# Two layers of a transformer block on one Trainium2 core: the second layer's weight conversions begin at step 28 and stay behind the step that asks for them

## The chip, the core and the metric

The kernel runs on one core of one Trainium2 chip. A core has five engines with a queue each, taken in order: TensorE (PE in the profile, with PEld for its weight loads), VectorE (DVE), ScalarE (ACT), GpSimd (POOL) and SyncE (SP). In this kernel SP and ACT also issue the DMA transfers. The metric is device time in microseconds (us), the median of a few executions; lower is better.

## The reference

A linear attention with a decayed state feeds two feed-forward layers, each with its own weights. All values are float32; the four weight matrices come as float64.

```
for t in range(S):
    state = alpha[:, :, t, :, None] * state + einsum('bhd,bhe->bhde', k[:, :, t], v[:, :, t])
    y[:, :, t] = einsum('bhd,bhde->bhe', q[:, :, t], state)
x = y as (B*S, H*D) = (3072, 384)
h = x @ moe_w_in;   g = h if h >= 1, 0 if h <= -1, else (h + 1)**2 / 4;   x = g @ moe_w_out
h = x @ moe2_w_in;  g = max(0.01 * h, h);                                 out = g @ moe2_w_out
```

Here B = 4, S = 768, H = 8, D = 48, and the hidden width is 2048.

## The kernel before

**Tiles and steps.** The 3072 tokens are 24 chunks of 128, and three chunks make a tile of 384 tokens, so a layer has 8 tiles. A tile of one layer is 16 steps, one for each 128 hidden columns. Layer 1 (layer 0 in the code) is steps 0 to 127, layer 2 is steps 128 to 255. In a step, `gemm_in` makes `h` with nine matmuls (line 451: three row blocks, and three passes each, since every operand is split in a high and a low part), the activation makes the two parts of `gg`, and `gemm_out`, three steps later, adds nine matmuls into three accumulators (line 490 in layer 1, line 492 in layer 2).

**The activation of a step in layer 1** goes round three engines: ACT lines 462 and 463 (read `h`, then square), DVE line 464 (compare with `h`), ACT line 468 (high part of `gg`), POOL line 469 (low part). There are two banks for `h`, so the first matmul of step i+2 waits for line 464 of step i; four buffers of `gg` stand between line 469 and `gemm_out`.

**The attention** of the chunks of the next tile is spread over the 16 steps of a tile. For each chunk: transposes (line 254), scans on DVE (line 269, then after four short instructions line 281), scores (line 320) and their mask on DVE (line 327), the output `y` (lines 365 and 367) and the state (line 341). Its PSUM banks are three in turn, so a score matmul waits until a bank's readers, a scan or a mask, are done. The later tiles of layer 1 have somewhat less of it, the last one and layer 2 none.

**The conversions.** The float64 weights come in 28 pieces a layer. A piece is loaded (line 160; for layer 2 issued on ACT), and converted with integer arithmetic: ACT lines 29 and 30, DVE lines 31 and 32, POOL line 35, DVE line 40. For layer 1 the result is split at once into the resident weights (lines 178 and 182). For layer 2 those weight buffers are still in use, so the converted piece is stored to DRAM (line 187, issued on ACT), and from the last tile of layer 1 on, as each weight buffer comes free, it is loaded again (line 194, on ACT, asked for from step 114) and split.

`tick(layer, n)` does one beat of this: the first part of piece n (`conv_a`: lines 29 to 35), the last part of piece n-1 (`conv_b`: line 40), the load of piece n+2, and the store of piece n-2. Three raw buffers and four `z` buffers carry it; the `z` buffers also take the loads of line 194. Hooks run a tick at a step: for layer 2 the first at step `MF` = 16, then one every `TICK1` = 3 steps.

**What sets the order.** On PE the order is the order of the code. On the other engines a scheduler sets it at build time from its own estimate of when each instruction could start: an instruction whose data it takes to be ready may be queued well ahead of the step in which the code asks for it. The order of a queue is then fixed, and an instruction that has to wait holds up all that stand behind it.

Of the kernel before, what the change touches and what calls it, by code (L numbers as in the profile page):

```python
# [7 lines left out]
F32 = mybir.dt.float32  # L8
# [4 lines left out]
ACTF = mybir.ActivationFunctionType  # L13
ALU = mybir.AluOpType

C = 128
HI, LO = 0, 1
# [45 lines left out]
def fast_path(ctx, tc, q, k, v, alpha, w1i, w1o, w2i, w2o, out, wz, in_range):  # L63
    nc = tc.nc
# [6 lines left out]
    MF = DFF // 128  # L71
# [2 lines left out]
    NCH = NT // C  # L74
    LAG = 3
    TICK1 = 3
    AHEAD = 1
    DQ = 3
    EB = 2
# [16 lines left out]
    op = ctx.enter_context(tc.tile_pool(name="op", bufs=1))  # L96
# [47 lines left out]
    def load_raw(layer, kind, g, i):  # L144
        src = wsrc[layer, kind]
        if kind == "i":
            n = MG * 128
            src = src[i * 128:(i + 1) * 128, g * n:(g + 1) * n]
        else:
            n = DM  # L150
            r0 = (g * MG + i) * 128
            src = src[r0:r0 + 128, :]
        t = rawp.tile([128, MG * 128], I64, tag="raw", name="raw")[:, :n]
        if kind == "i" and layer == 0:
            cols = slice(g * n, (g + 1) * n)
            r3 = KD * R + 32 * i
            (cq if layer else nc.sync).dma_start(out=t[:R], in_=wsrc[layer, kind][i * R:(i + 1) * R, cols])
            (cq if layer else nc.sync).dma_start(out=t[R:], in_=wsrc[layer, kind][r3:r3 + 32, cols])
        else:
            (cq if layer else nc.sync).dma_start(out=t, in_=src)  # L160
        raw[layer, kind, g, i] = t
# [3 lines left out]
    def conv_a(layer, kind, g, i):  # L165
        t = raw.pop((layer, kind, g, i))
        n = t.shape[1]
        z = zp.tile([128, MG * 128], I32, tag="z", name="z")[:, :n]
        half_done[layer, kind, g, i] = to_f32_first(nc, t, z, nc.gpsimd), z

    def conv_b(layer, kind, g, i):
        high, z = half_done.pop((layer, kind, g, i))
        to_f32_last(nc, high, z)
        zs[layer, kind, g, i] = z.bitcast(F32)
# [11 lines left out]
    def store_z(kind, g, i):  # L186
        cq.dma_start(out=wz[kind, g][i], in_=zs.pop((1, kind, g, i)))
# [9 lines left out]
    order = [(kind, g, i) for g in range(NG) for kind in "io" for i in range(KD if kind == "i" else MG)]  # L197
    NO = len(order)

    def tick(layer, n):  # L200
        if n < NO:
            conv_a(layer, *order[n])
        if 0 <= n - 1 < NO:
            conv_b(layer, *order[n - 1])
            if layer == 0:
                split_hi(0, *order[n - 1])
            if n + 2 < NO:
                load_raw(layer, *order[n + 2])
        if 0 <= n - 2 < NO:
            if layer == 0:  # L210
                split_lo(0, *order[n - 2], nc.gpsimd if n % LOP else nc.vector)
            else:
                store_z(*order[n - 2])

    def w_tile(layer, kind, g):
        if (layer, kind, g) not in W:
# [44 lines left out]
    def st_alpha(c):  # L261
        ps = transposed(c, 0)
        if c > 0:
            load_qka(c + AHEAD)
        kt = tp.tile([R, NP, C], F32, tag="kt", name="kt")
# [176 lines left out]
    def gemm_in(layer, j, m, n):  # L442
        N = n * C
        xt = xts[layer, j]
        w = W[layer, "i", m // MG]
        f0 = (m % MG) * 128
        h = ph.tile([128, 512], F32, tag="h", name="h")[:, :N]
        cnt = 0
        for kk in range(KD):
            for wl, xl in PASSES:  # L450
                nc.tensor.matmul(  # L451
                    h, w[:, wl, kk, f0:f0 + 128], xt[:, kk, xl, :],
                    start=cnt == 0, stop=cnt == 3 * KD - 1,
                )
                cnt += 1
        if m == MF - 1:
            xts.pop((layer, j))
        t = ep.tile([128, 384], F32, tag="t", name="t", bufs=EB)[:, :N]
        g = t
        gg = gp.tile([128, 2, 384], F32R, tag="gg", name="gg")[:, :, :N]  # L460
        if layer == 0:
            nc.scalar.activation(out=t, in_=h, func=ACTF.Relu, bias=half, scale=0.5)  # L462
            nc.scalar.activation(out=t, in_=t, func=ACTF.Square)  # L463
            nc.vector.scalar_tensor_tensor(out=g, in0=t, scalar=1.0, in1=h, op0=ALU.min, op1=ALU.max)  # L464
        else:
            nc.scalar.activation(out=t, in_=h, func=ACTF.Copy, scale=0.01)  # L466
            nc.vector.tensor_tensor(out=g, in0=h, in1=t, op=ALU.max)  # L467
        nc.scalar.activation(out=gg[:, HI], in_=g, func=ACTF.Copy)  # L468
        nc.gpsimd.tensor_tensor(out=gg[:, LO], in0=g, in1=gg[:, HI].bitcast(F32), op=ALU.subtract)  # L469
        gs[layer, j, m] = gg  # L470

    def gemm_out(layer, j, m, n):
        N = n * C
# [68 lines left out]
    def at(i, f):  # L542
        hooks.setdefault(i, []).append(f)
# [1 line left out]
    NA = len(tilesA) * MF  # L545
    lastA = NA - MF
    for n in range(3):
        at(MF - 3 + n, lambda n=n: load_raw(1, *order[n]))
    for n in range(NO + 2):
        at(MF + TICK1 * n, lambda n=n: tick(1, n))  # L550
    for n, (kind, g, i) in enumerate(order):
        free = lastA + MG * g + MG + (LAG if kind == "o" else 0)
        at(free + i - 2, lambda a=(kind, g, i): load_z(*a))
# [252 lines left out]
```

## Time and profile before

| | us |
|---|---|
| runs timed | 1044.44 (median of three, 1043.35 to 1045.16) |
| the profiled execution, its own time | 1045.02 |
| span of its trace, first to last instruction | 1043.3 |
| PE busy | 988.5 |
| DVE, ACT, POOL busy | 496.5, 491.6, 399.5 |
| first step of layer 1 begins | 48.4 |
| first step of layer 2 begins | 626.0 |

The span is the time inside the trace; 1.7 us lie around it. The rows further down are of this one execution. A group of instructions in them is named by the line of the kernel, the engine and what it writes and reads, as in "L464 DVE t<-t,h"; "idle before" is how long the engine stood still ahead of such instructions, and behind the arrow stands what ended it.

### The profile page before, as it was taken

Reading aid. Unit: us, or ns where it says so; the run is one execution under the profiler, and the core shown is the slowest. Engines: PE = TensorE matmul, PEld = TensorE weight load, DVE = VectorE, ACT = ScalarE, POOL = GpSimd, SP = SyncE. Lnnn points to the kernel's source line nnn. Section 1 sums busy time; section 2 is a strip of 40 time slices with the busy share of each in tenths; the row PEclk is TensorE's granted clock in tenths of the full one; section 3 lists DMA queues with packets and bytes.
Section 4 is the critical chain, followed back from the end, with each engine's and each line's share of the span. In section 5 each row is a group of like instructions: output and inputs, shape, how many; then the busy total and the mean of one; then the engine's idle time right before and its main releaser. Section 6 shows DMA issues by size and latency. Waiting matters only on the chain.

```text
span 1043.3 us, 15722 instructions
## 1 busy us (share of the span) xinstructions
PE 988.5 (95%) x5874; PEld 963.7 (92%) x5874; DVE 496.5 (48%) x965; ACT 491.6 (47%) x966; POOL 399.5 (38%) x402
## 2 busy tenths in 40 slices
PE   5589799879999999999999999999999999999997
PEld 4588689779999999999999999999999999999997
DVE  7999997886444445354442345241423212221211
ACT  4476666565444444445544674333333333333332
POOL 2477775564233333332222333333333333333332
PEclk9898999999999999999999999999999999999999
DMA  9855558766222121122110235020302000000000
GB/s 191 196 147 134 146 167 239 187 195 166 38 55 46 35 58 35 35 58 42 42 38 6 84 113 170 26 91 2 91 1 68 1 24 1 23 1 23 16 7 27
DMA packets 133652, 78.96 MB, mean 76 GB/s; under 512 B 104384, under 2 KB 122304, under 8 KB 133568
## 3 DMA queue, kind: packets, MB, share of 16 engines
q1 hardware_dynamic: 121472, 52.71, 20.9%
q10 hardware_dynamic: 12096, 25.17, 8.0%
q8 instruction: 48, 0.79, 0.3%
q14 instruction: 36, 0.29, 0.1%
HBM read 59.77 MB, written 15.73 MB: 72 GB/s over the span
## 4 chain that ended last, share of the span: by engine, by line
PE 74%; DVE 11%; DMA 6%; issue 3%; ACT 3%; POOL 2%; SPq 1%; ACTq 0%; POOLq 0%; DVEq 0%
PE h L451 33%; PE acc L492 18%; PE acc L490 14%; DMA raw<-in_moe_w_in 3%; PE y L367 3%; PE sc L320 2%; DVE z L40 2%; DVE z L31 2%; DMA raw<-in_moe_w_out 1%; POOL z L35 1%; PE y L365 1%; DVE z L32 1%; DMA ends<-in_alpha 1%; DVE kt L269 1%; DVE qt L281 1%
## 5 line engine op out<-in xcount | busy, mean ns | idle before, releaser
L451 PE MATMUL h<-xt,wi 128*128 128x384 f32 x2304 | 459.8, 343 | 15.3 <-DVE t L464 7.8
L469 POOL TENSOR_TENSOR gg<-t,gg 128x384 fp32r<-128x384 f32 x256 | 269.1, 1052 | 492.5 <-ACT gg L468 489.3
L451 PEld LDWEIGHTS h<-xt,wi 128*128 128x128 f32 x2304 | 405.9, 189 | 21.9 <-DVE t L464 10.9
L490 PE MATMUL acc<-gg,wo 128*128 128x384 f32 x1152 | 234.6, 347 | 1.9 <-ACT o L503 1.0
L492 PE MATMUL acc<-wo,gg 128*128 128x384 f32 x1152 | 223.5, 338 | 0.0
L468 ACT ACTIVATE gg<-t 128x384 fp32r<-128x384 f32 x256 | 133.6, 522 | 169.9 <-DVE t L464 92.2
L490 PEld LDWEIGHTS acc<-gg,wo 128*128 128x128 f32 x1152 | 202.3, 189 | 5.0 <-ACT o L503 1.3
L492 PEld LDWEIGHTS acc<-wo,gg 128*128 128x128 f32 x1152 | 205.1, 188 | 0.0
L467 DVE TENSOR_TENSOR t<-h,t 128x384 f32<-128x384 f32 x128 | 71.1, 557 | 272.6 <-ACT t L466 272.6
L466 ACT ACTIVATE t<-h 128x384 f32<-128x384 f32 x128 | 62.9, 492 | 180.0 <-PE h L451 178.7
L464 DVE SCALAR_TENSOR_TENSOR t<-t,h 128x384 f32<-128x384 f32 x128 | 70.0, 547 | 119.8 <-ACT t L463 117.3
L462 ACT ACTIVATE t<-h,half 128x384 f32<-128x384 f32 x128 | 73.6, 575 | 81.8 <-PE h L451 63.0
L35 POOL TENSOR_TENSOR z<-z,raw 128x384 int32<-128x384 int32 (+1 forms) x56 | 70.3, 1255 | 66.0 <-DVE z L32 21.3
L463 ACT ACTIVATE t<-t 128x384 f32<-128x384 f32 x128 | 66.8, 522 | 7.0 <-ACT t L462 2.9
L320 PE MATMUL sc<-qab,kt 96*128 96x256 f32 x192 | 53.6, 404 | 14.5 <-DVE S L327 7.4
L367 PE MATMUL y<-S,vpad 128*96 128x128 f32 x384 | 55.9, 272 | 5.6 <-DVE S L327 5.6
L40 DVE SCALAR_TENSOR_TENSOR z<-raw,z 128x384 int32<-128x384 int32 (+1 forms) x56 | 50.8, 909 | 9.8 <-POOL z L35 8.6
L320 PEld LDWEIGHTS sc<-qab,kt 96*128 96x128 f32 x192 | 36.8, 200 | 20.2 <-DVE S L327 9.0
L367 PEld LDWEIGHTS y<-S,vpad 128*96 128x96 f32 x384 | 46.4, 162 | 6.3 <-DVE S L327 6.3
L29 ACT ACTIVATE raw<-raw 128x384 int32<-128x384 uint32 (+1 forms) x56 | 34.0, 608 | 35.5 <-DMA raw<-in_moe_w_in 20.2
L301 ACT ACTIVATE qab<-qt,bdm 96x512 f32<-96x512 f32 x48 | 32.0, 714 | 19.0 <-DVE qt L295 19.0
L31 DVE TENSOR_SCALAR z<-z 128x384 f32<-128x384 f32 (+1 forms) x56 | 35.4, 633 | 9.6 <-ACT z L30 9.5
(69 smaller groups left out, 671.6 us busy)
## 6 DMA issues: line engine op xcount, KB each, us to landing
raw<-in_moe_w_out SPq DMA_DIRECT2D x16, 384.0 KB, 3.1
raw<-in_moe_w_in ACTq DMA_DIRECT2D x12, 512.0 KB, 4.5
raw<-in_moe_w_out ACTq DMA_DIRECT2D x16, 384.0 KB, 3.9
nat<-in_alpha SPq DMA_DIRECT2D x24, 192.0 KB, 3.5
nat<-in_k SPq DMA_DIRECT2D x24, 192.0 KB, 4.3
nat<-in_q SPq DMA_DIRECT2D x24, 192.0 KB, 4.4
vpad<-in_v SPq DMA_DIRECT2D x48, 96.0 KB, 2.6
raw<-in_moe_w_in SPq DMA_DIRECT2D x12, 384.0 KB, 4.7
```

Of the source, the lines that this page charges most:

```text
L35: add_eng.tensor_tensor(out=z, in0=z, in1=low, op=ALU.add)
L40: nc.vector.scalar_tensor_tensor(out=z, in0=high, scalar=-0x40000000, in1=z, op0=ALU.bitwise_and, op1=ALU.bitwise_or)
L320: nc.tensor.matmul(ps[:, i].rearrange("p e t -> p (e t)"), cs[c]["kt"][:, a, :], cs[c]["qab"][:, a].rearrange("p e t -> p (e t)"),)
L367: nc.tensor.matmul(y[:, a, :], vp[:, 2 * a + e, :], d["S"][:, a, e, :], start=first and e == 0, stop=e == 1)
L451: nc.tensor.matmul(h, w[:, wl, kk, f0:f0 + 128], xt[:, kk, xl, :], start=cnt == 0, stop=cnt == 3 * KD - 1,)
L462: nc.scalar.activation(out=t, in_=h, func=ACTF.Relu, bias=half, scale=0.5)
L464: nc.vector.scalar_tensor_tensor(out=g, in0=t, scalar=1.0, in1=h, op0=ALU.min, op1=ALU.max)
L467: nc.vector.tensor_tensor(out=g, in0=h, in1=t, op=ALU.max)
L468: nc.scalar.activation(out=gg[:, HI], in_=g, func=ACTF.Copy)
L469: nc.gpsimd.tensor_tensor(out=gg[:, LO], in0=g, in1=gg[:, HI].bitcast(F32), op=ALU.subtract)
L490: nc.tensor.matmul(acc[d][:, :N], w[:, wl, mi, d * 128:(d + 1) * 128], gg[:, xl], start=st, stop=sto)
L492: nc.tensor.matmul(acc[d][:, :DM], gg[:, xl, d * C:(d + 1) * C], w[:, wl, mi, :], start=st, stop=sto)
```

## The change

Two things. The layer-2 ticks begin at step `LATE1` = 2 * 16 - 4 = 28 in place of step 16, still one every three steps, so that the last first part (piece 27) is asked for at step 109 and the last store at step 115; the first three loads are asked for at steps 25 to 27 in place of 13 to 15. And each tick is traced inside `tc.issue_after(...)` for the three activation instructions of the latest traced step that the tick's engines run (DVE line 464, ACT line 468, POOL line 469): whatever the tick issues on one of these engines, its DMAs on ACT too, must stand behind that engine's instruction in the queue. The first three loads are outside of it.

```diff
+    LATE1 = 2 * MF - 4
...
+    step_ins = []
+
+    def tick1(n):
+        with ExitStack() as behind:
+            for ins in step_ins[-1]:
+                behind.enter_context(tc.issue_after(ins))
+            tick(1, n)
...
-            nc.vector.scalar_tensor_tensor(out=g, in0=t, scalar=1.0, in1=h, op0=ALU.min, op1=ALU.max)
+            gi = nc.vector.scalar_tensor_tensor(out=g, in0=t, scalar=1.0, in1=h, op0=ALU.min, op1=ALU.max)
...
-        nc.scalar.activation(out=gg[:, HI], in_=g, func=ACTF.Copy)
-        nc.gpsimd.tensor_tensor(out=gg[:, LO], in0=g, in1=gg[:, HI].bitcast(F32), op=ALU.subtract)
+        hi = nc.scalar.activation(out=gg[:, HI], in_=g, func=ACTF.Copy)
+        lo = nc.gpsimd.tensor_tensor(out=gg[:, LO], in0=g, in1=gg[:, HI].bitcast(F32), op=ALU.subtract)
         gs[layer, j, m] = gg
+        step_ins.append((gi.ins, hi.ins, lo.ins))
...
     for n in range(3):
-        at(MF - 3 + n, lambda n=n: load_raw(1, *order[n]))
+        at(LATE1 - 3 + n, lambda n=n: load_raw(1, *order[n]))
     for n in range(NO + 2):
-        at(MF + TICK1 * n, lambda n=n: tick(1, n))
+        at(LATE1 + TICK1 * n, lambda n=n: tick1(n))
```

No instruction of the work itself is added or removed, and PE's order is the same in both. In the changed kernel lines 160 to 194 are one higher, and lines 254 to 469 nine higher (461 to 464 and 468, for example, are 470 to 473 and 477). In the rows below, a name with a number is one tile (`h_1385` is the `h` of one step).

ScalarE at steps 14 and 15, the last two of the first tile, before: lines 462, 463 and 468 are a step's activation, lines 29 and 30 a layer-2 conversion, lines 160 and 187 its load and store.

```order
L462 ACTIVATE t_1395<-h_1385,half_118 128x384
L29 ACTIVATE raw_1383<-raw_1383 128x512
L30 ACTIVATE z_1615<-raw_1383 128x512
L463 ACTIVATE t_1395<-t_1395 128x384
L29 ACTIVATE raw_1411<-raw_1411 128x512
L30 ACTIVATE z_1754<-raw_1411 128x512
L462 ACTIVATE t_1423<-h_1413,half_118 128x384
L468 ACTIVATE gg_1396<-t_1395 128x384
L463 ACTIVATE t_1423<-t_1423 128x384
L160 DMA raw_1622<-in_moe2_w_out 128x384
L187 DMA wzi0_60<-z_1466 128x512
```

The same place in the changed kernel:

```order
L471 ACTIVATE t_1391<-h_1381,half_118 128x384
L472 ACTIVATE t_1391<-t_1391 128x384
L477 ACTIVATE gg_1392<-t_1391 128x384
L471 ACTIVATE t_1417<-h_1407,half_118 128x384
L472 ACTIVATE t_1417<-t_1417 128x384
L477 ACTIVATE gg_1418<-t_1417 128x384
```

The conversions, their loads and their stores have left this place, and the two steps stand alone.

ScalarE at the end of step 45 and the start of step 46, in the third tile, before:

```order
L463 ACTIVATE t_2858<-t_2858 128x384
L468 ACTIVATE gg_2859<-t_2858 128x384
L462 ACTIVATE t_2894<-h_2884,half_118 128x384
L463 ACTIVATE t_2894<-t_2894 128x384
L468 ACTIVATE gg_2895<-t_2894 128x384
```

and in the changed kernel, with one tick:

```order
L472 ACTIVATE t_2818<-t_2818 128x384
L477 ACTIVATE gg_2819<-t_2818 128x384
L29 ACTIVATE raw_2574<-raw_2574 128x384
L30 ACTIVATE z_2834<-raw_2574 128x384
L188 DMA wzo0_64<-z_2567 128x384
L161 DMA raw_2841<-in_moe2_w_in 128x512
L471 ACTIVATE t_2854<-h_2844,half_118 128x384
L472 ACTIVATE t_2854<-t_2854 128x384
```

Two activations, a store and a load have come between the last activation of one step and the first of the next.

VectorE at the scans of chunk 16, at the start of the fifth tile (names without their numbers), before: line 269 is the first scan, line 281 the second, line 327 the mask.

```order
L269 SCALAR_TENSOR_TENSOR kt<-Tal,zcol 96x127 x4
L274 TENSOR_TENSOR tot<-Tal,kt 96x4
L275 TENSOR_SCALAR tot<-tot 96x4
L276 RECIPROCAL rtot<-tot 96x4
L277 SCALAR_TENSOR_TENSOR good<-tot,good 96x4
L281 SCALAR_TENSOR_TENSOR qt<-Tal,rtot,zcol 96x128 x4
L327 TENSOR_TENSOR S<-sc,causal 128x512
```

and in the changed kernel:

```order
L40 SCALAR_TENSOR_TENSOR z<-raw,z 128x384
L278 SCALAR_TENSOR_TENSOR kt<-Tal,zcol 96x127 x4
L283 TENSOR_TENSOR tot<-Tal,kt 96x4
L31 TENSOR_SCALAR z<-z 128x384
L284 TENSOR_SCALAR tot<-tot 96x4
L32 TENSOR_SCALAR z<-z 128x384
L285 RECIPROCAL rtot<-tot 96x4
L286 SCALAR_TENSOR_TENSOR good<-tot,good 96x4
L290 SCALAR_TENSOR_TENSOR qt<-Tal,rtot,zcol 96x128 x4
L336 TENSOR_TENSOR S<-sc,causal 128x512
```

The three passes of a tick on VectorE have come in front of and into the chain of the scans. Of the chains from chunk 7 on, six have passes of a tick in or right before them in this way (chunks 11, 14, 16, 18, 20 and 23); in the kernel before, those of chunks 7 to 10 had.

## Rows read from the trace of the kernel before

**Rows 1.** The page: TensorE's busy tenths in 40 slices of 26 us.
```profile
PE   5589799879999999999999999999999999999997
```

**Rows 2.** Stretches (us, length): busy us (instructions) of each engine; granted clock, DMA share, GB/s.
```profile
128.00:137.32 9.32, 8.87 (x51) 7.96 (x49) 8.32 (x13) 6.14 (x12) 8.03 (x7) 1.00 0.63 184
137.32:220.90 83.58, 74.70 (x457) 69.06 (x457) 68.89 (x136) 52.46 (x107) 50.57 (x47) 1.00 0.74 202
220.90:297.50 76.60, 72.22 (x460) 69.59 (x458) 44.47 (x94) 40.09 (x79) 29.94 (x33) 1.00 0.40 106
297.50:368.44 70.94, 70.94 (x459) 69.66 (x457) 33.65 (x75) 33.80 (x65) 21.93 (x25) 1.00 0.22 47
368.44:439.40 70.96, 70.96 (x460) 69.67 (x457) 33.67 (x75) 33.79 (x65) 21.94 (x25) 1.00 0.22 47
```

The engines stand in the order PE, PEld, DVE, ACT, POOL.

**Rows 3.** TensorE's groups, 137.3 to 297.5 us: busy us, mean ns; idle before.
```profile
L451 PE MATMUL h<-xt,wi 128*128 128x384 f32 x289 | 59.1, 348 | 7.5 <-DVE t L464 7.5
...
L320 PE MATMUL sc<-qab,kt 96*128 96x256 f32 x48 | 12.6, 385 | 1.7 <-DVE S L327 1.7
```

**Rows 4.** TensorE's groups of instructions from 297.5 to 439.4 us.
```profile
L451 PE MATMUL h<-xt,wi 128*128 128x384 f32 x289 | 58.8, 347 | 0.0
...
L320 PE MATMUL sc<-qab,kt 96*128 96x256 f32 x48 | 12.3, 378 | 0.0
```

**Rows 5.** Whom TensorE waited for, 137.32 to 297.5 us (total us, times, longest).
```profile
PE h L451 <- DVE t L464: 7.5, 8, 2.1
PE sc L320 <- DVE S L327: 1.7, 3, 0.7
```

**Rows 6.** ScalarE's groups of instructions, 137.32 to 243 us.
```profile
L29 ACT ACTIVATE raw<-raw 128x384 int32<-128x384 uint32 (+1 forms) x26 | 15.7, 604 | 17.4 <-DMA raw<-in_moe_w_out 10.2 <-DMA raw<-in_moe_w_in 7.2
L30 ACT ACTIVATE z<-raw 128x384 f32<-128x384 f32 (+1 forms) x26 | 15.2, 586 | 0.0
```

**Rows 7.** The conversions on VectorE, 137 to 243 us (ns min/median/max; first, last).
```profile
L40 DVE SCALAR_TENSOR_TENSOR z<-raw,z x28: 523/680/1550, 138.2 to 242.6; 128x384 int32<-128x384 int32 x16, 128x512 int32<-128x512 int32 x12
L32 DVE TENSOR_SCALAR z<-z x27: 341/408/1196, 137.2 to 240.8; 128x384 int32<-128x384 int32 x16, 128x512 int32<-128x512 int32 x11
L31 DVE TENSOR_SCALAR z<-z x26: 342/409/1673, 138.9 to 240.1; 128x384 f32<-128x384 f32 x16, 128x512 f32<-128x512 f32 x10
```

**Rows 8.** The page: GpSimd's part of the conversions.
```profile
L35 POOL TENSOR_TENSOR z<-z,raw 128x384 int32<-128x384 int32 (+1 forms) x56 | 70.3, 1255 | 66.0 <-DVE z L32 21.3 <-PE ktok L309 14.2 <-DMA nat<-in_alpha 5.5
```

**Rows 9.** In order of time, end of step 45 to start of 48 (start us, us).
```profile
291.29 0.53 ACT L468 ACTIVATE gg<-t 128x384 fp32r<-128x384 f32 x1 [0.69 <-DVE t L464]
291.89 1.02 POOL L469 TENSOR_TENSOR gg<-t,gg 128x384 fp32r<-128x384 f32 x1 [2.85 <-ACT gg L468]
...
292.63 0.58 ACT L462 ACTIVATE t<-h,half 128x384 f32<-128x384 f32 x1 [0.81 <-PE h L451]
...
293.87 0.56 DVE L464 SCALAR_TENSOR_TENSOR t<-t,h 128x384 f32<-128x384 f32 x1 [2.61 <-ACT t L463]
...
297.48 1.30 PE L451 MATMUL h<-xt,wi 128*128 128x384 f32 x6
```

**Rows 10.** The second scans of chunk 16 and the scores behind them, in order of time.
```profile
371.31 1.59 DVE L281 TENSOR_TENSOR_SCAN qt<-Tal,rtot,zcol 96x128 f32<-96x128 f32 x4
...
374.58 1.03 PE L320 MATMUL sc<-qab,kt 96*128 96x256 f32 x4
```

**Rows 11.** The same of chunk 17.
```profile
393.63 1.59 DVE L281 TENSOR_TENSOR_SCAN qt<-Tal,rtot,zcol 96x128 f32<-96x128 f32 x4
...
395.60 1.03 PE L320 MATMUL sc<-qab,kt 96*128 96x256 f32 x4
```

**Rows 12.** DMA issues by line (count, size of one, median us to landing).
```profile
raw<-in_moe_w_in ACTq DMA_DIRECT2D x12, 512.0 KB, 4.5
...
wzo<-z ACTq DMA_DIRECT2D x16, 192.0 KB, 4.8
```

**Rows 13.** The issue of a `wzo` store on ScalarE's queue (ns min/median/max).
```profile
L187 ACTq DMA_DIRECT2D wzo<-z x16: 326/400/1189, 152.5 to 243.2; - x16
```

More of the change, by code (lines that the diff above doesn't have):

```diff
@@ L463, in gemm_in @@
             nc.scalar.activation(out=t, in_=t, func=ACTF.Square)
-            nc.vector.scalar_tensor_tensor(out=g, in0=t, scalar=1.0, in1=h, op0=ALU.min, op1=ALU.max)
+            gi = nc.vector.scalar_tensor_tensor(out=g, in0=t, scalar=1.0, in1=h, op0=ALU.min, op1=ALU.max)
         else:
             nc.scalar.activation(out=t, in_=h, func=ACTF.Copy, scale=0.01)
-            nc.vector.tensor_tensor(out=g, in0=h, in1=t, op=ALU.max)
-        nc.scalar.activation(out=gg[:, HI], in_=g, func=ACTF.Copy)
-        nc.gpsimd.tensor_tensor(out=gg[:, LO], in0=g, in1=gg[:, HI].bitcast(F32), op=ALU.subtract)
+            gi = nc.vector.tensor_tensor(out=g, in0=h, in1=t, op=ALU.max)
+        hi = nc.scalar.activation(out=gg[:, HI], in_=g, func=ACTF.Copy)
+        lo = nc.gpsimd.tensor_tensor(out=gg[:, LO], in0=g, in1=gg[:, HI].bitcast(F32), op=ALU.subtract)
         gs[layer, j, m] = gg
+        step_ins.append((gi.ins, hi.ins, lo.ins))
     def gemm_out(layer, j, m, n):
```

## The prediction

> **What bounds the kernel now.** I first read the busy slices [rows 1]: from the tenth slice (234.7 us) on, TensorE's digit is 9 up to the last one, and it is lower only before. So where TensorE is full, an edit on the other engines gains nothing; what can be gained lies in the first 235 us. Next the stretches [rows 2], cut where a tile of layer 1 begins. The fourth and fifth tile (297.50 to 439.40 us) take 70.94 and 70.96 us, and TensorE is busy in all of it. The second takes 83.58 us and the third 76.60. Is that more work? The groups of instructions say no: from 137.3 to 297.5 us TensorE runs 289 matmuls of line 451 and 48 of line 320 [rows 3], and just as many from 297.5 to 439.4 us, where nothing waits [rows 4]. So two tiles lose time in waiting, and in starting again behind each wait.
>
> What they wait for is mostly line 464 on VectorE, 7.5 us in 8 waits, and after that the mask of the scores, 1.7 us [rows 5]. In that stretch VectorE is busy 68.89 of 83.58 us against 33.65 of 70.94 in the fourth tile [rows 2]. The difference is the layer-2 conversions: 28 last passes between 138.2 and 242.6 us [rows 7], about one for each step, where the code asks for one in three. On ScalarE the same pieces have another price: line 29 stood 17.4 us waiting for raw weights to land [rows 6], and every activation queued behind it stood too.
>
> **The change part by part.** *Conversions out of the second and third tile.* The order of ScalarE at steps 14 and 15 has them no longer, and the ticks begin at step 28, the thirteenth of the second tile. If both tiles then run as the fourth and fifth, with the same instructions on TensorE, they take 141.90 us in place of 83.58 + 76.60 = 160.18 [rows 2]: 18.3 us less. Nothing is late next in those tiles: it is TensorE itself that fills the fourth and fifth. Before 137.32 us a few conversions go too; TensorE stood 9.32 - 8.87 = 0.45 us there [rows 2], so that gives 0 to 0.45, and I take 0.2, since layer 1's own conversions stand there as well.
>
> *The same conversions put into tiles that have none.* None of their work is saved. A tick is lines 29 and 30 (0.60 + 0.59 us [rows 6]), a store and a load issued on the same queue (0.40 us for the store [rows 13]; I take the same for the load), lines 31, 32 and 40 on VectorE (0.41 + 0.41 + 0.68 us at their medians [rows 7]) and line 35 on GpSimd (1.26 us [rows 8]). The cover is thinnest in steps with no attention between them, as 45 to 48 [rows 9]. There ScalarE ends step 45's line 468 at 291.82 and begins step 46 at 292.63. With a tick between them, which the order puts just there, it is free at 291.82 + 1.19 + 0.80 = 293.81, so step 46 begins 1.2 us later, and its line 464 ends at 295.6 in place of 294.43. TensorE needs that bank at 297.48. So 1.9 us of cover are left. VectorE's line 31 starts when line 30 is done, at 293.01, and with line 32 is done at 293.8, before step 46 needs VectorE (295.05); with both at their longest (1.67 + 1.20 us [rows 7]) it is done at 295.9, and line 464 ends at 296.4, still ahead of 297.48. GpSimd ends line 469 at 292.91, has line 35 from 293.8 to 295.1, and step 46's line 469 would come at about 296.2. SP issues nothing of a tick. A load issued two ticks, that is six steps, ahead of its use has some 6 x 70.9 / 16 = 26 us to land in, where 4.5 is the median [rows 12], so the 17.4 us of waiting have no reason to come back. I put the ticks as such at 0. From below a gain is excluded, since TensorE is already full there; from above the bound is the price that the same conversions have now, 18.3 / 28 = 0.65 us each, which would be all of the gain.
>
> *Passes in the chain of the scans.* Six chains of scans (chunks 11, 14, 16, 18, 20, 23) get passes of a tick. In chunk 16 the second scans end at 372.90 and the scores that may need their bank begin at 374.58, 1.68 us later [rows 10]; in chunk 17, and the others whose number leaves the same rest by three, it is 395.22 to 395.60, 0.38 us [rows 11]. Three passes at their medians are 1.50 us. That is under 1.68, and 1.12 over 0.38, for four chains (11, 14, 20, 23) 4.5 us. From below it is 0: in four of the six the order puts the mask (line 327) ahead of the second scans, and the scores may then take the bank that the mask sets free. Between the ends lies what such chains cost now: chunks 7 to 10 have even more passes among them and the scores waited 1.7 us in all [rows 5], 0.43 for each. Six times that is 2.6; there are fewer passes now, and I take half, 1.3 us.
>
> These passes would also meet GpSimd more regularly. The longest line 31 takes 1.67 us and the shortest 0.34 [rows 7], a difference about as long as a pass on GpSimd (1.02 to 1.26 us [rows 8, 9]). The Trainium skill, in "SBUF — State Buffer", section "Who interferes with whom", says that VectorE and GpSimd share one pair of SBUF ports, that an instruction which takes the pair holds it to its end, and that the other stands still for that long. That speaks against the change, which queues a tick beside the GpSimd pass of the same step; by it the sum would have one GpSimd pass more in each chain, as the second case below has it. By the medians, which hold whatever blocking there is now, it has none.
>
> *The end of layer 1.* The loads of line 194 use the `z` buffers of the conversions. Before, they could be issued once the last conversion was through, near 243 us; now the last store is asked for at step 115 and the first reload at 114. The third reload stands on ScalarE behind the landing of a store issued shortly before: 4.8 us at the median [rows 12], with lines 463 and 468 (0.53 us for the latter [rows 9], and I take the same for both) in between, so ScalarE could stand up to 3.7 us, 0.7 more than the 3.05 us between line 464 and the next use of its bank [rows 9]; for two such places 0 to 1.4 us. The 4.8 us was measured with the DMA engines busy for 0.74 of the second tile; in the fourth tile, which has less traffic as the end has, it is 0.22 [rows 2], so I take 0.3.
>
> Sum: -18.3 - 0.2 + 0 + 1.3 + 0.3 = -16.9 us. The profiled execution took 1045.02 us, so it would take 1028.1. The median of the runs is 0.58 us under that execution, so I give 1044.44 - 16.9 = **1027.5 us**.
>
> **The rivals.** *The chains pay.* VectorE's passes are held up in the six chains, by GpSimd or by their place. With three passes at the medians and one GpSimd pass of 1.02 us more, four chains lose 1.12 + 1.02 = 2.14 and two lose 1.50 + 1.02 - 1.68 = 0.84: 10.2 us in place of 1.3, that is 1036.4 us. By the port rule of the skill this is the case to expect; that chunks 7 to 10 lost only 1.7 us, among more passes, speaks against it.
>
> *A backlog stays.* VectorE is busy 8.32 of 9.32 us ahead of the second tile [rows 2], so the second tile might start late and keep half of its 12.6 us: 1033.8 us. Against it: the third tile loses nothing more after its last conversion (242.6 us [rows 7]), as the digits show [rows 1].
>
> *The price travels.* Each conversion costs 0.65 us wherever it stands, and the time is 1044.4. That the change doesn't do what it says would end there too, but the order of the queues rules that out. Against both: the 3.05 us of cover.
>
> *Slower.* The load of a tick needs the raw buffer that line 40 of the same tick sets free, so ScalarE stands at that load until VectorE has run it, and with it the next step's line 462. If VectorE comes to line 40 only after a scan or a mask, ScalarE is held beyond the 1.9 us of cover left. It decides from 0.65 us for each of the 28 ticks, that is from some 2.5 us of standing each time; at 0.9 it is 28 x 0.9 = 25 us against 18.3, about 1051 us. Against it: in the order line 40 stands right behind line 464 almost everywhere, and 0.68 us is less than the 1.19 us of lines 29 and 30.
>
> **How the numbers follow.** Chances: the forecast (up to 4.5 us in the chains) 0.72; the chains pay 0.10; a backlog stays 0.08; the price travels or nothing happens 0.05; slower 0.05. The low end is a full gain of 18.75 us from the median, 1025.7, less 0.8 for the spread of the runs: 1024.9. The high end has to leave out no more than 0.2: it reaches to the backlog's 1033.8 and stops short of the others, 1034. About 0.2%, 2 us, is what a measurement of this kernel can tell from no change. All cases but the last two are faster by more: 0.90; within 0.05; slower 0.05.
>
> **What would show it.** Right: the second and third tile each take about 71 to 73 us with TensorE's digits at 9 from the sixth slice or so; no wait of line 451 for line 464 after 137 us; line 29 waiting for no landing; lines 31, 32 and 40 spread from about 185 to 570 us. The chain term shows as waits of line 320 for VectorE at six places, the reload term as a wait near step 113. Wrong: tiles from the third on longer than before, with line 451 waiting for line 464 behind each tick, or a second tile still at 80 us with no conversion in its first twelve steps.

## The result, and the profile after

The changed kernel takes 1026.3 us (median of four executions, 1026.2 to 1027.6), the kernel before 1044.8 in the same comparison: a ratio of 0.983, with an interval from 0.981 to 0.984. The gain is 18.5 us, where 16.9 were forecast. The traced execution is the one of 1027.6 us; its span is 1026.0 us, 17.3 less than before.

TensorE's busy tenths in 40 slices, now of 25.65 us, from the page of the changed kernel; they answer to [rows 1]:

```profile
PE   6688799999999999999999999999999999999997
```

The digit is 9 from the sixth slice on, where it had been from the tenth. The stretches of the changed kernel, cut where a tile of layer 1 begins (columns as in [rows 2]):

```profile
128.00:137.10 9.10, 8.27 (x48) 7.59 (x46) 5.43 (x9) 5.50 (x11) 7.76 (x7) 1.00 0.68 189
137.10:208.00 70.90, 70.90 (x460) 69.62 (x457) 36.08 (x80) 35.99 (x70) 23.73 (x28) 1.00 0.24 52
208.00:279.00 71.00, 71.00 (x460) 69.71 (x457) 39.19 (x90) 38.25 (x75) 28.52 (x31) 1.00 0.39 95
279.00:349.90 70.90, 70.90 (x458) 69.62 (x457) 41.06 (x90) 38.50 (x75) 28.34 (x30) 1.00 0.37 93
```

The second and third tile had 83.58 and 76.60 us [rows 2]; now each takes 71, and TensorE is busy in all of it. The fourth has ticks for the first time and is no longer than it was. VectorE has 36 to 41 us of work in each of these tiles, where it had 69, 44 and 34. From 137.1 us to the end TensorE waits in one place only (total us, times, longest), at the start of layer 2:

```profile
PE h L460 <- DVE t L476: 2.2, 2, 1.2
```

ScalarE's part of the conversions from 137.1 to 560 us, which answers to [rows 6], and VectorE's, which answers to [rows 7] (lines 30 and 32 are left out):

```profile
L29 ACT ACTIVATE raw<-raw 128x384 int32<-128x384 uint32 (+1 forms) x28 | 16.7, 597 | 0.0
```

```profile
L40 DVE SCALAR_TENSOR_TENSOR z<-raw,z x28: 543/552/1108, 204.9 to 558.8; 128x384 int32<-128x384 int32 x16, 128x512 int32<-128x512 int32 x12
...
L31 DVE TENSOR_SCALAR z<-z x28: 325/418/513, 194.0 to 549.2; 128x384 f32<-128x384 f32 x16, 128x512 f32<-128x512 f32 x12
```

At line 29 ScalarE waits for no landing at all, where it stood 17.4 us, and the conversions lie over 365 us in place of 104. They also run shorter than before: the longest line 31 takes 0.51 us, and took 1.67.

### The profile page after: what moved, and what is told of

It reads as the page before. It is cut to its first block, busy times and chain, and to the rows that moved or that the text cites. A ratio compares the mean times of both kernels' runs of the same rounds, so it can differ in the third digit from the quotient of the medians.

```text
span 1026.0 us, 15727 instructions
## 1 busy us (share of the span) xinstructions
PE 985.7 (96%) x5874; PEld 965.3 (94%) x5874; DVE 483.3 (47%) x965; ACT 492.0 (48%) x966; POOL 397.6 (39%) x402
## 4 chain that ended last, share of the span: by engine, by line
PE 86%; DVE 6%; DMA 3%; issue 2%; POOL 1%; ACT 1%; SPq 1%; POOLq 0%; ACTq 0%; DVEq 0%
PE h L460 37%; PE acc L502 19%; PE acc L500 18%; PE sc L329 3%; PE y L376 3%; PE y L374 2%; DVE z L40 1%; DMA raw<-in_moe_w_in 1%; PE kv L350 1%; DMA ends<-in_alpha 1%; POOL z L35 1%; DVE z L31 1%; PE Tal L263 1%; PE Tq L263 1%; DVE good L528 1%
## 5 line engine op out<-in xcount | busy, mean ns | idle before, releaser
L40 DVE SCALAR_TENSOR_TENSOR z<-raw,z 128x384 int32<-128x384 int32 (+1 forms) x56 | 44.6, 796 | 3.9 <-POOL z L35 1.6
L29 ACT ACTIVATE raw<-raw 128x384 int32<-128x384 uint32 (+1 forms) x56 | 33.7, 602 | 17.3 <-DMA raw<-in_moe_w_in 12.9
L31 DVE TENSOR_SCALAR z<-z 128x384 f32<-128x384 f32 (+1 forms) x56 | 30.5, 544 | 22.8 <-ACT z L30 22.6
L278 DVE TENSOR_TENSOR_SCAN kt<-Tal,zcol 96x127 f32<-96x127 f32 x96 | 32.4, 396 | 14.1 <-PE Tal L263 14.1
```

## The experiments

### Which of the two edits does it

**The later start alone.** The ticks begin at step 28, and nothing keeps them behind a step:

```diff
-        at(LATE1 + TICK1 * n, lambda n=n: tick1(n))
+        at(LATE1 + TICK1 * n, lambda n=n: tick(1, n))
```

> The ticks are asked for from step 28, but without the rule that keeps them behind the activation. The queues of all engines come out word for word as in the kernel before: the scheduler pulls the conversions to the same places. Theory 'order in the queues': the time of before, 1044.8 us within 0.2%. Theory 'the later start': about 1026 us, since the code asks for them at step 28. If it comes out at the time of before, asking later does nothing by itself.

Measured: 1045.5 us beside 1045.3 for the kernel before, ratio 1.000 (0.999 to 1.001). The scheduler undoes the later start: a load that is asked for at step 25 and whose buffer is free goes to the same place as ever, and its conversion with it. The later start changes no instruction's place: in the two traces the queues of all engines have the same order.

**The rule alone.** The ticks begin at step 16, as before, and are kept behind their steps:

```diff
-    LATE1 = 2 * MF - 4
+    LATE1 = MF
```

> The ticks are asked for from step 16 as before, one every three steps, each kept behind the activation of its step. Theory 'order in the queues': the second tile (steps 16 to 31) has 5 ticks as the later tiles have, takes 71 us, and the time is 1026.3 us, within 1 us. Theory 'the later start': the conversions of the second tile still meet what layer 1's own conversions leave behind and their loads, so the second tile keeps its 12.6 us and the time is about 1039 us.

Measured: 1026.07 us, ratio 0.982 (0.980 to 0.983), the whole gain. The second tile takes 70.9 us with five ticks in it:

```profile
136.90:207.80 70.90, 70.90 (x458) 69.62 (x457) 40.27 (x92) 39.48 (x78) 28.99 (x32) 1.00 0.35 88
```

**The rule on ScalarE alone.** The tick is kept behind line 477 and not behind the lines of VectorE and GpSimd:

```diff
-        step_ins.append((gi.ins, hi.ins, lo.ins))
+        step_ins.append((hi.ins,))
```

> The changed kernel, but each tick is kept behind the activation of its step on ScalarE alone (line 477), not on VectorE and GpSimd. What VectorE and GpSimd have of a tick depends on ScalarE's lines 29 and 30 anyway. Theory 'ScalarE's queue is what counts': 1026.3 us within 0.3%, and the second and third tile 71 us. Theory 'VectorE's queue counts by itself' (lines 31, 32 and 40 in the scheduler's own places there): part of the 18 us comes back, most where line 40 is put ahead of an activation, 1030 us or more.

Measured: 1028.0 us, ratio 0.984 (0.982 to 0.985), beside 1027.4 for the changed kernel on the same chip; every tile from the second to the fifth takes 70.96 us. ScalarE's activations come out in the same order as in the changed kernel and VectorE's queue does not, so that VectorE's order was tested too: to place the tick on ScalarE is enough, since the rest of it depends on lines 29 and 30.

### How dense, or in what order

**One tick in every step, with the rule.**

```diff
-    TICK1 = 3
+    TICK1 = 1
```

> The ticks start at step 28 and stay behind the activation of their step, but one comes in every step, as many per step as the kernel before had: 28 conversions in steps 28 to 55. Theory 'order in the queues': each tick costs as little as now, tiles two to four take 71 us each and the time is 1026 to 1028 us. Theory 'density' (VectorE and ScalarE have room for one conversion in three steps, not for one in each): the 18 us are lost again, in the third and fourth tile, and the time is about 1044 us.

**A floor and no more.** Every tick is kept behind step 27's activation, and from there the scheduler places it:

```diff
-            for ins in step_ins[-1]:
+            for ins in step_ins[LATE1 - 1]:
```

> Every tick is kept behind the activation of step 27, and behind no later one: the conversions cannot come before step 28, but from there the scheduler puts them where it likes, which is 28 conversions in steps 28 to 46, mostly inside the activation chains. Theory 'order in the queues': the loss comes back, 28 x 0.65 = 18 us, now in the third tile, so about 1044 us. Theory 'the later start': 1026 us, since layer 1's own conversions and their loads are over by then (the DMA share is 0.22 there in place of 0.74). Between them: the part of the 18 us that was the waiting for raw weights to land (ScalarE stood 17.4 us for it before) is gone and the part of the order stays.

Measured: one in every step 1029.9 us, ratio 0.985 (0.984 to 0.987), some 2 us over what was expected for the order and 14 under what was expected for density; with a floor alone 1045.3 us, ratio 1.000 (0.999 to 1.001): all is lost again, in other tiles. The stretches of the two, each with its three tiles from the second on; first one tick in every step, then the floor:

```profile
138.50:209.50 71.00, 71.00 (x460) 69.72 (x458) 40.04 (x85) 37.69 (x74) 26.46 (x29) 1.00 0.28 65
209.50:281.30 71.80, 71.26 (x459) 69.59 (x457) 57.03 (x122) 47.87 (x98) 41.52 (x41) 1.00 0.69 196
281.30:352.50 71.20, 71.20 (x459) 69.55 (x457) 45.29 (x101) 40.73 (x82) 32.51 (x34) 1.00 0.49 135
```

```profile
137.00:212.20 75.20, 71.75 (x459) 69.50 (x457) 45.82 (x90) 38.30 (x77) 28.29 (x31) 1.00 0.32 75
212.20:297.60 85.40, 76.11 (x459) 72.09 (x457) 69.35 (x142) 54.38 (x110) 50.09 (x48) 0.96 0.74 211
297.60:368.50 70.90, 70.90 (x458) 69.61 (x457) 35.89 (x77) 34.08 (x66) 23.99 (x27) 1.00 0.28 66
```

With one tick in every step the DMA share is 0.69 and VectorE has 57 us of work in a tile, and the two tiles lose 1.2 us together. (Of the 3.9 us by which this run is over the one with the rule alone, 1.6 lie ahead of the second tile, which began at 138.5 us and not at 136.9; no conversion of layer 2 stands there.) With the floor two tiles lose 18.7 us. In the second of them the granted clock fell to 0.5 (1.2 GHz in place of 2.4) for two stretches of 3.4 us, from 269.8 and from 293.7 us, each 1.0 to 1.4 us after TensorE had waited 3.2 and 2.5 us; at half the clock that makes some 3.4 us of the 18.7, by estimate. In the kernel before, the clock was 1.00 in both tiles [rows 2]. ScalarE's line 29 in the two, from the step-28 tick to the last, in the same order:

```profile
L29 ACT ACTIVATE raw<-raw 128x384 int32<-128x384 uint32 (+1 forms) x28 | 16.8, 598 | 0.0
```

```profile
L29 ACT ACTIVATE raw<-raw 128x384 int32<-128x384 uint32 (+1 forms) x28 | 17.0, 609 | 17.8 <-DMA raw<-in_moe_w_in 11.4 <-DMA raw<-in_moe_w_out 6.1
```

The 17.8 us of standing come back with the scheduler's own order, long after layer 1's conversions and their loads have ended, so layer 1's loads were not the cause. Nor is it the DMA engines' share by itself: one tick in every step has a share of 0.69 and no standing. It is the distance between a load and its use. In the kernel before, a load lands 4.2 us after its issue (median over the 28) and ScalarE is free for line 29 after 3.8 us, so that it stands and begins at 4.4. With the rule line 29 begins 8.2 us behind the issue at one tick in a step, and 26.9 at one in three. One doubt stays: left alone, the scheduler packs 28 conversions into steps 28 to 46, some 1.5 in a step, where the rule had one. How much of the 18.7 us is that closer packing, how much the place within a step, and how much the fallen clock, no run here separates.

**A buffer more, with the old order.** If the landing were all, a fourth raw buffer and a load asked for one tick earlier should do as well, in the kernel before:

```diff
-    rawp = ctx.enter_context(tc.tile_pool(name="rawp", bufs=3))
+    rawp = ctx.enter_context(tc.tile_pool(name="rawp", bufs=4))
...
-            if n + 2 < NO:
-                load_raw(layer, *order[n + 2])
+            if n + 2 + layer < NO:
+                load_raw(layer, *order[n + 2 + layer])
...
-    for n in range(3):
-        at(MF - 3 + n, lambda n=n: load_raw(1, *order[n]))
+    for n in range(4):
+        at(MF - 4 + n, lambda n=n: load_raw(1, *order[n]))
```

> The kernel before with a fourth raw buffer, and each layer-2 load asked for one tick earlier. Nothing is kept behind anything. Theory 'the landing': ScalarE stood 17.4 us at line 29 because a load was issued 4.4 us (median) ahead of its use and takes 3.8 us to land; with a buffer more the distance grows, these waits go and with them most of the 18 us: about 1030 us. Theory 'order in the queues': the scheduler uses the buffer to put the conversions still further ahead (in the order the first one comes in step 10 in place of 13), behind a load again, so ScalarE stands there as before: about 1045 us.

Measured: 1053.9 us, slower: ratio 1.008 (1.006 to 1.009). Neither theory had this. The first two tiles, and ScalarE's line 29 from 125 to 240 us:

```profile
52.40:152.60 100.20, 80.61 (x431) 74.68 (x431) 93.70 (x154) 63.78 (x131) 75.58 (x63) 0.87 0.62 159
152.60:234.80 82.20, 75.03 (x460) 70.64 (x457) 68.12 (x135) 52.51 (x107) 52.15 (x46) 0.98 0.72 214
```

```profile
L29 ACT ACTIVATE raw<-raw 128x384 int32<-128x384 uint32 (+1 forms) x28 | 16.9, 605 | 3.5 <-DMA raw<-in_moe_w_in 2.5 <-DMA raw<-in_moe_w_out 0.8
```

The standing at line 29 shrinks to 3.5 us (one wait more, 3.3 us at line 468, is put down to such a landing), and the loss grows all the same. The scheduler used the buffer to start at step 10, among layer 1's own conversions, and the first tile takes 100.2 us, with VectorE busy 93.7 of them, where it had taken 88.9 (48.4 to 137.32 us) with 84.2. So the landing was a symptom. What costs is that conversions are queued ahead of the activations that TensorE waits for, whether they stand there or work there.

### What is left over a tick

**One copy more, and two longer ones.** In each tick ScalarE copies a tile `pad` of 1152 columns onto itself (or twice one of 1728), behind lines 29 and 30:

```diff
...
             tick(1, n)
+            for _ in range(1 if n < NO else 0):
+                nc.scalar.activation(out=pad, in_=pad, func=ACTF.Copy)
```

> The changed kernel with one more instruction on ScalarE in each of the 28 ticks: a copy of a 128x1152 tile onto itself, behind lines 29 and 30 and ahead of the next step's first activation; nothing else reads it. A copy of this width takes 1.17 us in this kernel. It measures the cover over a tick. In the changed kernel the bank of a step with a tick is set free 1.44 to 6.8 us before TensorE needs it (at step 46 still 3.05 us, as before, where the prediction had left 1.9). Theory 'the tick ran in ScalarE's idle time': the copy takes 1.2 us of the 3.05, TensorE waits nowhere, 1026.3 us within 0.3%, and line 460 waits less than 0.5 us in all. Theory of the prediction (1.9 us left in tight steps, less in the tightest): also no wait at step 46, but up to 0.9 us at one or two places, 1027 us. If the cover is nearly used up already, 28 x 1 us are lost: 1050 us.

> The same with two copies of a 128x1728 tile onto itself in each tick, some 3.5 us (1.17 us for 1152 columns, half as much again, twice). That is more than the cover of 3.05 us at step 46 and of the other tight steps. By the cover as the changed kernel's trace has it, TensorE waits at the 9 or 10 ticks with less than 3.5 us left, for 7 to 8 us in all: about 1034 us. By the prediction's account, with 1.15 us less left behind each tick, it waits at about 20 of them for 20 us: about 1046 us. If ScalarE is not what sets the end of these steps, 1026 us.

Measured: one copy 1026.4 us, ratio 0.982 (0.980 to 0.983), and TensorE waits nowhere between the second tile and layer 2. Two copies 1035.5 us, ratio 0.991 (0.989 to 0.992), near the 1034 expected from the cover in the changed kernel's trace. A copy of 1152 columns took 1.16 us and one of 1728 took 1.64, so the cover over a tick lies between 1.2 and 3.3 us at the tightest places. Whom TensorE waited for with two copies, from 137 us to the end of layer 1 (four lines are added, so line 504 is line 500 of the changed kernel, 517 is 513, 464 and 477 are 460 and 473):

```profile
PE acc L504 <- ACT o L517: 3.3, 3, 1.6
PE h L464 <- DVE t L477: 1.7, 2, 0.8
```

That the time came near to the expectation is luck. Of the 7 to 8 us of waits for line 477 that were expected, only 1.7 came, at two places. The larger wait is for the copies of the finished accumulators at the end of a tile, which stand in ScalarE's queue too and which the expectation had not counted.

**GpSimd's pass twice.** A second addition in each tick (`more` is 1 for layer 2 and 0 for layer 1), into words that nothing reads afterwards:

```diff
...
     add_eng.tensor_tensor(out=z, in0=z, in1=low, op=ALU.add)
+    for _ in range(more):
+        add_eng.tensor_tensor(out=low, in0=z, in1=low, op=ALU.add)
```

> The changed kernel with a second pass of GpSimd in each of the 28 ticks: behind line 35, the same integer addition into the low words of the raw tile, which nothing reads afterwards, 1.02 to 1.3 us each. It tests whether VectorE's short instructions in the chain of the scans are held up by GpSimd. In the changed kernel the instruction that takes 0.12 us at its shortest (line 286) takes 1.7 to 2.0 us in chunks 14, 16 and 18 and ends within 0.05 us of a GpSimd pass. Theory 'GpSimd holds VectorE': with one pass more queued at these places the chains whose scores had 0.2 to 0.4 us left (chunks 14, 16, 17, 20) end up to 1 us later and TensorE waits at line 329, 1 to 4 us in all: 1027 to 1030 us, and the mean of line 286 rises. Theory 'no hold': VectorE's instructions keep their times, TensorE waits nowhere, 1026.3 us.

Measured: 1027.5 us, ratio 0.983 (0.982 to 0.985), too near to the changed kernel for the times to tell; the trace tells. Chunk 23 of this run in order of time (line 288 is line 286 of the changed kernel, 295 is 293, line 37 the added pass):

```profile
514.43 0.82 POOL L295 TENSOR_TENSOR state<-state,tot 96x384 f32<-96x384 f32 x1
514.48 2.74 DVE L288 SCALAR_TENSOR_TENSOR good<-tot,good 96x4 f32<-96x4 f32 x1
515.21 1.00 POOL L480 TENSOR_TENSOR gg<-t,gg 128x384 fp32r<-128x384 f32 x1
516.17 1.02 POOL L37 TENSOR_TENSOR raw<-z,raw 128x384 int32<-128x384 int32 x1
517.14 0.68 DVE L338 TENSOR_TENSOR S<-sc,causal 128x512 f32<-128x512 f32 x1
517.87 1.13 PE L331 MATMUL sc<-qab,kt 96*128 96x256 f32 x4 [0.31 <-DVE S L338]
```

An instruction on 96x4 numbers takes 2.74 us, through three passes of GpSimd one behind the other, and ends at 517.22; the added pass ends at 517.19. In the changed kernel, without that pass, the same one took 1.76 us. TensorE then waits 0.31 us for the mask behind it. In chunk 14 the added pass holds line 286 of this run (284 of the changed kernel) for 1.04 us in place of 0.17, and TensorE waits 0.47 us for the scans behind it. These two waits, 0.8 us, are all there are before layer 2, a little under the 1 to 4 us expected. GpSimd holds VectorE, for the length of its passes.

### A version that goes further

The one wait that is left is at the start of layer 2. There the changed kernel's VectorE has, in order of time:

```profile
623.29 0.55 DVE L476 TENSOR_TENSOR t<-h,t 128x384 f32<-128x384 f32 x1
625.32 5.13 DVE L528 TENSOR_REDUCE good<-ends 128x1 f32<-128x1152 f32 x4 [1.49 <-DMA ends<-in_alpha]
...
630.97 1.84 PE L460 MATMUL h<-xt,wi 128*128 128x384 f32 x9 [1.21 <-DVE t L476]
```

It is the same fault once more: four reductions that the code asks for in steps 153 and 163 are queued 20 to 30 steps early, ahead of the activations, and behind a load. With the ticks from step 16, and with the reductions asked for three steps after their load and kept behind that step's activation:

```diff
...
+    def alpha_red(e):
+        t = ends_t.pop(e)
+        with tc.issue_after(step_ins[-1][0]):
+            for i, op in enumerate((ALU.max, ALU.min)):
+                col = NP + i * NE + e
+                nc.vector.tensor_reduce(out=good[:, col:col + 1], in_=t, op=op, axis=mybir.AxisListType.X)
...
+        at(NA + MF + (e * 5 * MF) // NE + 12, lambda e=e: alpha_red(e))
```

> A version meant to beat both: the ticks begin at step 16 and are kept behind their step (1026.07 us as measured), and the two reductions of alpha (line 528 of the changed kernel) are asked for three steps after their load and kept behind the activation of that step on VectorE, where now the scheduler puts them 20 steps early, so that VectorE stands waiting for their load at the start of layer 2. If that standing is what makes layer 2's first tile 53.42 us in the changed kernel (51.93 with the ticks from step 16) against 50.67 for the later ones, the tile takes 50.7 us, the wait of line 460 for line 476 goes, and the time is 1.2 us under 1026.1: 1024.9 us. If not, the tile stays at 52 us and the time at 1026.

Measured: 1025.8 us, ratio 0.981 (0.979 to 0.982). The tile takes 50.67 us and TensorE waits for nothing from 139 us to the end; but this traced execution had begun its first tile at 51.6 us, 3.4 later than the changed kernel's. So both were run again, on one chip:

> The changed kernel as it is, beside the next one: 1026.3 us, with layer 2's first tile at 52 to 53.5 us.

> The version with the ticks from step 16 and the reductions of alpha kept behind their step, once more, beside the changed kernel on the same chip. Its trace had no wait of TensorE from the second tile to the end, so layer 2's first tile takes 50.7 us, 1 to 2.5 us less than in the changed kernel: 1024 to 1025.5 us. The start of the program varies by up to 3 us from one traced execution to the next, so the medians may lie within 1 us of each other.

Measured: the changed kernel 1027.4 us, ratio 0.983 (0.981 to 0.984); the further version 1024.55 us, ratio 0.980 (0.978 to 0.981). On this chip it is 2.8 us faster, some 0.3%. The tile accounts for 1.6 us of that (52.28 and 50.67 in these two traces); the rest is no more than the start of the second tile varies by (136.9 to 139.0 us). Against the rule alone from step 16 (1026.07 us, on another chip) no gain in time is shown, since the intervals of the two ratios overlap. Layer 2's first tile in the changed kernel's first trace, then in the further version:

```profile
607.40:660.90 53.50, 51.28 (x291) 50.64 (x290) 22.33 (x32) 21.68 (x43) 16.91 (x16) 1.00 0.30 96
```

```profile
608.00:658.70 50.70, 50.70 (x290) 50.70 (x290) 14.95 (x26) 21.70 (x43) 17.02 (x16) 1.00 0.20 66
```

## Why the prediction was right, step by step

**The two tiles, -18.3 us:** right. They went from 83.6 and 76.6 us to 70.9 and 71.0, 18.3 us together. Of the reason that the prediction gave, that the conversions stood about one in a step and ahead of the activations, the runs bear out the place: with one in every step, but kept behind the activations, the tiles lose 1.2 us. That they begin later, which the prediction had not told apart from that, does nothing by itself.

**Before 137.32 us, -0.2:** cannot be told. The second tile began 0.2 us earlier, but over all executions traced here, the one with a buffer more left out, it began between 136.9 and 139.0 us. TensorE's standing between 128 us and the second tile, on which the term rested, did not shrink: it was 0.45 us [rows 2] and is 0.83 (9.10 less 8.27).

**The ticks, 0:** right, with a working that charged too much. The prediction had ScalarE occupied 1.19 + 0.80 us for a tick and the tight step 46 begin 1.2 us later. The changed kernel in order of time, at that very place (here and below, rows of other instructions in between are left out):

```profile
272.77 0.53 ACT L477 ACTIVATE gg<-t 128x384 fp32r<-128x384 f32 x1 [0.69 <-DVE t L473]
272.78 0.33 ACTq L188 DMA_DIRECT2D wzo<-z  x1
273.20 0.53 ACT L29 ACTIVATE raw<-raw 128x384 int32<-128x384 uint32 x1
273.24 0.74 ACTq L161 DMA_DIRECT2D raw<-in_moe_w_in  x1
273.64 0.54 ACT L30 ACTIVATE z<-raw 128x384 f32<-128x384 f32 x1
274.11 0.58 ACT L471 ACTIVATE t<-h,half 128x384 f32<-128x384 f32 x1
...
275.36 0.55 DVE L473 SCALAR_TENSOR_TENSOR t<-t,h 128x384 f32<-128x384 f32 x1 [0.34 <-ACT t L472]
...
278.96 1.30 PE L460 MATMUL h<-xt,wi 128*128 128x384 f32 x6
```

The store is issued while line 477 runs, the load while lines 29 and 30 run: on this queue an issue took no time from the activations beside it. Line 30 follows line 29 after 0.44 us, though each is listed with 0.53. So lines 29 and 30 take 0.98 us together, and line 471 begins 0.81 us after line 477 has ended (273.30 to 274.11), just as line 462 had behind line 468 [rows 9]: the tick went into time in which ScalarE had stood idle. Line 473 ends at 275.91, 3.05 us ahead of the next use of its bank, as before. None of the cover went.

**The chains of the scans, +1.3:** too much, it was 0, and this is the term that was mis-sized most. The prediction read 0.38 us behind the scans of four chunks [rows 11] (chunk 11, one of them, had 0.15) and let 1.50 us of passes eat it. Its own counterweight, that the mask may come first and free a bank, is what happened in half of the six chains: in chunks 11, 18 and 23 the scores begin 0.51, 0.92 and 0.96 us before the second scans have ended, so they did not wait for those. Chunk 18 in the changed kernel:

```profile
397.41 1.59 DVE L290 TENSOR_TENSOR_SCAN qt<-Tal,rtot,zcol 96x128 f32<-96x128 f32 x4
...
398.07 1.03 PE L329 MATMUL sc<-qab,kt 96*128 96x256 f32 x4
```

In chunk 14 all three passes run ahead of the first scan, and the chain is as before, with 0.27 us left (it had 0.38). Chunk 20, in the kernel before:

```profile
462.84 0.82 POOL L284 TENSOR_TENSOR state<-state,tot 96x384 f32<-96x384 f32 x1 [2.95 <-DVE tot L275]
462.89 1.76 DVE L277 SCALAR_TENSOR_TENSOR good<-tot,good 96x4 f32<-96x4 f32 x1
463.62 1.01 POOL L469 TENSOR_TENSOR gg<-t,gg 128x384 fp32r<-128x384 f32 x1
464.57 1.60 DVE L281 TENSOR_TENSOR_SCAN qt<-Tal,rtot,zcol 96x128 f32<-96x128 f32 x4
...
466.56 1.03 PE L320 MATMUL sc<-qab,kt 96*128 96x256 f32 x4
```

and in the changed kernel, with one pass of the tick, line 40, in the chain (lines 31 and 32 come behind the scans):

```profile
443.87 0.55 DVE L40 SCALAR_TENSOR_TENSOR z<-raw,z 128x384 int32<-128x384 int32 x1
444.59 1.03 POOL L478 TENSOR_TENSOR gg<-t,gg 128x384 fp32r<-128x384 f32 x1 [3.23 <-ACT gg L477]
444.82 0.81 DVE L286 SCALAR_TENSOR_TENSOR good<-tot,good 96x4 f32<-96x4 f32 x1
445.56 0.68 DVE L336 TENSOR_TENSOR S<-sc,causal 128x512 f32<-128x512 f32 x1
445.58 0.82 POOL L293 TENSOR_TENSOR state<-state,tot 96x384 f32<-96x384 f32 x1
...
446.16 1.59 DVE L290 TENSOR_TENSOR_SCAN qt<-Tal,rtot,zcol 96x128 f32<-96x128 f32 x4
...
448.02 1.03 PE L329 MATMUL sc<-qab,kt 96*128 96x256 f32 x4
```

The short instruction took 1.76 us through two passes of GpSimd one behind the other (lines 284 and 469) and ended with the second (464.65 and 464.63). Now line 478 comes first, and the short instruction takes 0.81 us and ends with that one pass (445.63 and 445.62). The chain had a hold of some 1.6 us inside it already; line 40 and the mask went into it, and the scans end 0.27 us ahead of the scores (447.75 to 448.02) in place of 0.39. In all 17 chains from chunk 7 on, in both kernels, this instruction ends 0.01 to 0.02 us after a pass of GpSimd; the shortest of all chunks takes 0.12 us. That is the rule of the Trainium skill, "SBUF — State Buffer", section "Who interferes with whom", that VectorE and GpSimd lock one pair of ports against each other, and the trace agrees.

The rival built on that rule was half right. In chunks 16 and 18 the GpSimd pass of the tick (line 35) did lengthen the hold, from 0.79 to 1.69 and 1.97 us, that is by 0.9 and 1.2 us, where the rival had charged 1.02 on top of the passes. It cost nothing even so: in chunk 16 the time behind the scans fell from 1.68 us [rows 10] to 0.22, still above zero, and in chunk 18 the scores did not wait for the scans.

**The reloads at the end of layer 1, +0.3:** too much, it was 0. The waits that ScalarE's queue shows in front of a reload (line 195) took 38 ns at most, and the stores' landing, which the term rested on, fell from 4.8 us [rows 12] to 1.9:

```profile
L195 ACTq EVENT_SEMAPHORE  x9: 17/17/38, 472.1 to 603.0; - x9
```

```profile
wzo<-z ACTq DMA_DIRECT2D x16, 192.0 KB, 1.9
```

**The sum.** The forecast started from the traced execution, and there the span fell by 17.3 us: 18.3 in the two tiles and 0.2 before them, less 0.6 in layer 2's first tile (52.8 to 53.4 us) and 0.5 behind the start of the last tile (60.3 to 60.9). So the 1.3 + 0.3 us that came to nothing were nearly made up for by 1.2 us that the forecast did not name, and that 16.9 came so near is in part luck. The 18.5 us is the difference of two medians. Those 1.2 us are no cost of the change: layer 2's first tile, with its waits of 2.2 us, takes 53.4 and 52.3 us in two traced executions of the changed kernel, and 52.8 and 52.9 in two with the old order, and the last part takes 60.3 to 60.9 us over all executions traced.

**The rivals.** *The price travels* is what the floor showed: in both places where the scheduler put the conversions by itself they cost some 18 us. Begun at the same step, but kept behind the activations, they cost 0 to 1.2. *A backlog stays* and *slower* fell with the second tile's 70.9 us and the unchanged cover of step 46.

## What to carry to other kernels

Where a scheduler fills in-order queues by the time at which work could start, a later request for side work and more buffers for it move nothing, or move it further ahead; what helps is to tie that work behind the instruction that the busy engine waits for. The slack in front of a wait is not only what lies behind the last instruction of a chain: a short instruction with a long duration inside it can be slack too, and in chunk 20 work put there cost nearly nothing. It is not free where the side work brings a GpSimd pass that lengthens the hold, as in chunks 16 and 18. Look for the same fault at the next place (here the reductions) once the first is mended.

## What the runs showed beside that

A wait costs more than its length. In the kernel before, the two tiles lost 18.3 us while TensorE stood still for 13.3 of them [rows 2], with the clock at 1.00. With two copies per tick TensorE waited 5.0 us between the second tile and layer 2, and these tiles lost 8.5. In the seventh tile the granted clock was 0.98 where it is else 1.00, and the matmuls of line 504 had a mean of 356 ns, against 345 without the copies:

```profile
495.20:565.30 70.10, 68.33 (x405) 66.39 (x405) 33.01 (x73) 50.21 (x82) 24.23 (x25) 0.98 0.23 69
```

That is one stretch, 508.2 to 511.6 us, at 0.50, which began 0.7 us after TensorE had waited 1.5 us; by estimate it is 1.7 of the 3.5 us. What the rest is, no run separates.

The issue of a transfer on ScalarE ran beside its activations at step 46, 0.74 us of it between 273.24 and 273.98, and held up none of them. And a transfer's landing does not follow the DMA engines' share alone: the stores of `wzo` took 4.8 us in the kernel before and 4.3 with the floor (share 0.74 where they stood), but 2.3 with one tick in every step (0.69), and 1.9 in the changed kernel. What sets it, no run separates.
